# Turning 256 rows of the last layer on TensorE, and storing the last tile from ScalarE's queue

## The chip, the cores and the metric

The kernel runs on one core of a Trainium2 chip. The metric is the device time of one execution in microseconds (us); the time before is 461.48 us, the median of 3 runs (460.27 to 465.0). The core has TensorE (matmuls and weight loads, results in PSUM), VectorE, ScalarE and GpSimd (elementwise work, GpSimd also the gathers), and SyncE, which only issues transfers. Every engine works through its own queue in order and waits for others by semaphores.

## What is computed

Three layers, each working on the output of the one before. The first is a recurrent attention over 2 x 8 heads, 768 steps, with 40 channels a head. The second is a mixture of 8 experts over the 1536 tokens of 320 channels, two experts for each token. The third, the last, is a dense layer with an exponential unit:

```python
def _moe2_ref(x, w_in, w_out) -> np.ndarray:
    h = x @ w_in
    alpha = 1.0
    g = np.where(h > 0.0, h, alpha * (np.exp(np.minimum(h, 0.0)) - 1.0))
    return (g @ w_out).astype(np.float32)
```

Here x is 1536 x 320, w_in 320 x 2048 and w_out 2048 x 320, all fp32. The experts have 1024 hidden channels each and a relu.

## The kernel before

All large products are made of fp16 halves: a number is split into a high and a low part, and two or three products of parts are summed in PSUM (`PASSES`, L112, for the first matrix of a layer; L951, L952 and L954 for the second).

The attention runs in 12 tiles of 128 tokens (`attention`, L643). Each tile ends in `token_rows` (L620), which splits its rows, stores them to `x_rows` in DRAM and computes the router's logits. `router` (L771) makes tables of the rows that each expert takes. `expert` (L965) runs 16 times (8 experts, 2 halves of the tokens): gathers of rows `xg`, a turn to `xT` with channels on the partitions (`turn_row`, L587), the first product (`contract`, L938), relu and split, the second product (`second`, L940), and a store of `yo` to `y_rows`.

The last layer works on 6 blocks of 256 tokens (`last_layer`, L1130). For each block, `mixed` (L1109) takes two tiles of 128 tokens: two gathers of the experts' rows (`yg`, L1116), a weighted sum `x3` (L1121 on ScalarE, L1122 on VectorE), a split into `x3r` (`split_row`, L580: the high part L388, L389 or L391, the low part in two instructions, 64 and 256 columns, L403), and a turn into `x3T`. `ffn_in` (L1141) then multiplies by w_in, 8 groups of 16 matmuls (a pair of 128 hidden channels for 256 tokens, a PSUM bank each; three banks go round), and takes the unit on ScalarE (L1153 to L1155) and VectorE (L1156, L1157), with a split into `gh` and `gl_`. `ffn_out` (L1166) multiplies by w_out, for each tile 4 groups of 12 matmuls of 0.136 us, scales the result on VectorE (L1172, `zo`) and stores it (L1174).

Turning rows has two ways in `turn_row`. One is a transfer that transposes, on SyncE's queue (L590). The other, with `on_pe`, is five transposes of 128x128 on TensorE into a PSUM tile `T` (L594) and one copy of 128x640 into the destination, on VectorE (L378) or ScalarE (L379). The attention's tiles and the first three expert jobs take the second way, the last layer the first.

The order of the work is not that of the program text. Each call of `do` only records an operation (a group of instructions of one engine, with what it reads and writes and the engines that could do it). `do.run(ORDER)` (L1229) then issues all of them in the order of a compressed table, `ORDER` (L73 to L110), whose entries are the operation's number and which of its engines does it. Waits between engines follow from the buffers. So every engine's queue is a part of that list, and an engine that waits for one operation holds up all that stand behind it in its queue.

At the end, a flag says if the routing went over the tables' sizes; every engine loads it (L1233) and takes a branch (L1235) over a fallback, which is not run with these inputs. SyncE then waits for all transfers and engines (L1409).

Of the kernel before, what the change touches and what calls it, by code (L numbers as in the profile page):

```python
# [70 lines left out]


ORDER = """  # L73
c-jTQeFVCBf&lR6{r&y<KJVY>siC8#rJ<#vrK33w{n4G4e)LC6OFvo~IvN`KqobvvrJ<ptrJ<prqop7H(bCe;($LV-(T|pfj*gCohWmW7D1tBufkcrS5<|
LZ97!N~w2t)9B$7hXh=OF09Fj-ENDFBr5bGl)B#AbV4w6O(=ot9`%OZVrffkS`RzxCL6{#Rw^c~tmhUf_0p<{H9F0nE)K@;c-&0zzijQxPduqm3y;#dMZq
HA=4ZO{T%#Ye~qO=2tTcUTIWAa#6$t+6xO!2f}zu`6~#=SUN&;6?0;R<RrQd+dh(7s}vUY=`|X_AP2753GxbcpWQYdu)a*kRqz!DHI{r$PZWz2l&U>6MJD
c4)F$t;CHl%e}Wyc0senz3xDBLJd6`~1b?DUtd0LS#t>iOEo_Ah5rPniHa5becnt4gF(QtCi>HYlvO(Ts1EPaZkr-M+=eR<2@sEivHpYj<0-xXse2ITZ0O
EyyfsKhha$~c^3eOQX5l2VFl*kijBtZ}uf+^%0x5*8@B4)%EPZDJm5`Yx2zYrC4PE5%p{spdLJN(x;ME;0x2uP-g0ud${Y>zL9K6XL|*p^rlcVt40up*Jh
f53-WiO8Wxyi82Uf5Df?KM^x>N96DnnZ>K<37?aB@)rca_QV0%BEKR3nVev0>WqiU3tqsBWQ5F+4t7DtSRStsHS|Cni4$=qzQK;j8@x&!$Qkx~;);~WESV
!O#0{wv|4x+2zms$9N8*OJh$e9(DkOr|(K}JX?|7T3k}2x9_yftH58_F5hzA}eYvdCzpa}T~f+SxEfhuT^_#?rPG4e_-$U2#$8l*^em@d;}GSrQXlUb_I4  # L80
45G^V#dsbnKCnG&Irh_$P@XVyps>IMzyIY@+2?hN92+`Pzz?ste7>kVOHdk`VZ<;>Wb&7E(MS+BcOG9O<t%YbEX>TiK)>|dPANW20c*?`oe6<7l}|;hM>N
n8Wcens3ujU7z&^^4e2}kBA#rE5~#nCEZropRG$jdC8|sb^o<ImE%bYGKt<@!Nr*;Jg;MD|#V}2@P2QLm-KOu%gHo6W^E;|TJ}H73QZMGobjcUnCTw&>b?
7b~r2##n$JCrQD4Tjq#pnt3XBtv}q6rRR1*S(LT$~P52|7XnrbqYbDK#LMw9QQDDLtbJHc2ZS!+u46N&8HU`H=aR3NsNTMX%^NwWj;zh-{;28l@x5f)dyV
yP{&$pU4E0WKzt}RFsLLU(p}aQHtR<be4wPj!AG)F3qI5Exn`n^q$Gl2YN{f+>!o}>Yy1W%jB3mQ(#W?nNCm}D#;}&z@@k_m!}K#n);5)a2NUw^9fgCcGR
3J(ce>LMq#h?jegL-r7LuWsWNpY!o}DIbEgl?fqim6(QoM(_o7jzNH>|!nK)Nt;%tIVvNpHk2tLK8*$kUyb8Mb1utj#kmDnX$W-Dxo%W-+`#g#dfuW(hi$
`!aZ2iO`{=eFE|Tk$p4X6r1&Z}|qh<BD8^YjJ0;#~!&R*Jn4}fW2{hZpgN|2H)d4+=v~sCvL)aIg!6`Q})V@xI4Gz<9vdDa0_<M&e*^5JHE-c`97!cEgtY
ae#v(D72D;L{E)Z#6u)Q3-1q#1hkTfy^G#L}`+S;@@B==|$M_MS;ivqVKk!+e5WeJ+!h$aeGoBHa{MX!(PYJe|=hMQJ%kgFY!V5x$Zwm!JBb@j%|KN}8mC
p(}AukjJASwbBhg@B(3Nx-Kl!b{<5#I1Mp)NFpt<V&1e2KsFO|d7m*rXU1fzTJ;@-@CC41_h?5uSWkc=3o35o{qNMumqs6z0N6fb2p@iDO|YOof?{7FR+<
Y=}3ZB}T=ya1b^^R@@0k;Uwh5I=>eS(q1?V8@4IM#JK1S3GpdhgqL_?U&2**ig#fxO~jt~OCc`w#fN~1Q?bnsL_(a2Eh#TDVpuqdZLuQ?Vn;fNXYnE)#jD
sA%hF9mq>a>-%Hme)OLws-m861L6cchqs)$1oN^ixev=(DhNvuk3sV9x3urv}Q(pVfwHE}1^q`EYf=Hf;iOAC>ZQu0umNHZxeHKc_!ml)}tBuE2!C7q?Qe  # L90
32&dRT|1SNs)kLO9^2rkK}jaOukEq{GGUzH}YIw$O-8oo#glOR^G`O>C7gjm3)=c@>;&gH~B7SB|=Wh5BVuSB}92ijJ%gS>_I-5zm^19Q1;S6ddVx1P^xl
Cww0lBlp~6w9Ho;~lNlu^#gvS!$YHrI1EnlOWu#1$l@e7d@>rQFK#s_HIj$s>nUa-r@?6;}e^z$lQdui$X{T(Ij1pD~@>$s{2gQ+(N>L`%s2o)r@`bIdHz
lcLm6MWFE=o$dD-R_vrInbRS8{4o-K$rnpfu%*vSpvj&kCY8R7EW+KxI@xwN<E=l#ZNGKTsp;=Q5O&YD%ptCp9j&)P_=1>WZz!)VNw!(&|+$s$KaDIirTP
zMNG{YE$VbZMCeP)r*=}59(3<AN8(w)Sfz2*Jf9Js0Fp6LhY@JXc4Wiw&j5;XgzJDKDC<qx$;zB>R2T-M4zZ#rKil*qPEee>P+n`bFHMU)ugsj7iv`NYm7
Efx~!@VwUJiV1{%=DT1rc62koU1`b3**ZKa~Ew6!+V7TQKD>Pu~_{Y`7>F)gd@^sau^GFn{QYYFYBU9_vVR8Lw?%WF5SpaK1^J+zWu)+_o}t?Db))}h|kz
tC%XT_5Njy|3@ot-jY8UC?8CRU7MyKGY|mp^x;L-qgR=n_5_}X>t8it)WHqmbTQR`dn{oS9S(ET0&pxQ+=Ul^@E-S8IT1@{iv_?6gcT;od6g8s^|2So&z_
%tCc_+<Us)x0RyU_3@Ts>1fYPl{?PAw8_dB|CyczFGcx*1FBptb19h+f2xx#MP>j#O5v;)m0MG)!5R4vxMjxEO0OXAh*n%!7n_(krtiT!AM$t$ZF=GhAY}
$wzGvhx&1nhtfq5y)bc>!@_Z?ug)IDlV*IQYm&fH4Szl(95c#@y%_CF2Sn;9*pawXrZZ#&<?RFB@IsWbBNy(J-FiU|fu&@uQJ3YDUGV8%^T|vc}Co%)8MK
5#}HiVJl|Ocp5eHW&8{nQ#4zKZH|n-5oHw<m=QB-#!P75LD>A#h?^;MY$VLDjjWk8b7sp-n;COx<jsQl#w?kLF*WXH*Q}cxb8GI*y?HdRX4~wTJ@aAq&4&
3j2c}{Ht86#TmpL>MYiy28+nSpTvtkn#V?pZ!D`G`0!HQXJdt%0|s@=8oR>DeJDXU=B>`(2Jc{Yny$F5s_Yib^xroDI4R>tbtC2MY#t%{Yk-dZ)QZ|AJL)  # L100
3jPv!;0JQ%#}H?2KLY%*$sPWjjXoSvBp-{T38dSXSM9Tm9_8I(pp(Z>l<rrZLF=eV-MEMI$39HXI-oxEyaFX4-42YD`AiAo3*x&PR>r+w*7FR9kwGjViR`
Mj@c8NwWs#U5$uh<wfFYip4kigz4Ojq*@$ztcXr->ItM#thn<Uawf}B2&c#02H+yCh&da&m4?E-iWGjx~ylmh&4s;53*-1O7dod#p=|-KHleUMUxRdsZ_S
jiEZD-<SoUD^@l1|>qIjk$VCHqI`=A@jPS#v5*)hRe{oRYJ0rjFvq-LltpvR=ojJAJ3;G@P7gyK`9aK63^Ra9hsM3A+h*<Ya8<rre18uU^tEdTS@@rro?d
bL#Hgjky`O=oZ|n_la9}Yu+B_+~0U5ujE$T1$^t)y_VZ>n{M0fxLvpJZk(DscLwgzJ;1%Ybhl2=UAQB633txIX?UM`D|hXV-HAJOkFe#<+@rg3zjF`n+1<
HOPx0>V$$h#HH|AYj#9P6aOL&YYcvtu4p5R~LUm@_?-q`DTT`%t0-rDPUeQ)4><;}d27YU}`#Cs1n-rU=IdoSUgJ?J5D=PkVN;00dc!CQJ^FC1LFh_~{t-
rY-jH!mGLJOVQC=!Ibfo;(5m<h{HojKgS<^3re!+pr8{FaeWLfw2HU8$y_cDY%0-n1MN%hXoi9im(JLunI@;4wFG0*5DI9U;}1@Uj>NYfpNbJ75@dBumv*
#;j_Nr+dlBaKJ+7g%KwEQ^Amp3Px~1^>*s=;|8GGt7{k2ZgA-Wv>wdv6`z62OSNykr%dh!OzwP&7$DhJNPzw6~+~4~{f8-DRu|M$#@DF~^|HhyBD}U+VeI
{7=Yk%XP{D*(=xBkvQ`l&z&%0WA*1>@lCU;IkY397-5{>`rk-JlUPgH|vNdciE{2a{kB%!99jQLqT!1?%AHE5SL~1>0a1Y=V7o2#!HI^zuP~gs#CQK!Q^+
gLZHaZowmX2IWvV)C>tBCNv7Yf=Y-8wL;O55&|J2a6&K?3B^M3P$KkEC>5%PvY||<9fH9)lndoUh0vQ&DO3w}LiJE1)D87Q{}1NZS84
"""  # L110
# [1302 lines left out]
```

## Time and profile before

| | |
|---|---|
| median of 3 runs | 461.48 us (460.27 to 465.0) |
| the profiled execution, its time | 461.11 us |
| its span, first to last instruction | 459.3 us |
| TensorE matmul busy | 436.1 us (95%) |
| VectorE busy | 382.2 us (83%) |
| ScalarE busy | 299.1 us (65%) |
| GpSimd busy | 95.9 us (21%) |
| mean granted TensorE clock | 0.99 |

A row of the trace names a line of the kernel, an engine (PE is TensorE's matmuls, PEld its weight loads, DVE VectorE, ACT ScalarE, POOL GpSimd, SP SyncE; a q behind the name is the engine's queue, as DMA issues, waits and branches), the operation, the tiles it writes and reads, and shapes. Idle time in brackets stands before the row's instruction, with what ended it. A line such as L388 or L403 is that of a helper and stands for many places.

### The profile page before, as it was taken

Reading aid. Unit: us, or ns where it says so; the run is one execution under the profiler, and the core shown is the slowest. Engines: PE = TensorE matmul, PEld = TensorE weight load, DVE = VectorE, ACT = ScalarE, POOL = GpSimd, SP = SyncE. Lnnn points to the kernel's source line nnn. Section 1 sums busy time; section 2 is a strip of 40 time slices with the busy share of each in tenths; the row PEclk is TensorE's granted clock in tenths of the full one; section 3 lists DMA queues with packets and bytes.
Section 4 is the critical chain, followed back from the end, with each engine's and each line's share of the span. In section 5 each row is a group of like instructions: output and inputs, shape, how many; then the busy total and the mean of one; then the engine's idle time right before and its main releaser. Section 6 shows DMA issues by size and latency. Waiting matters only on the chain.

```text
span 459.3 us, 10628 instructions
## 1 busy us (share of the span) xinstructions
PE 436.1 (95%) x4128; PEld 369.8 (81%) x4128; DVE 382.2 (83%) x845; ACT 299.1 (65%) x525; POOL 95.9 (21%) x105
## 2 busy tenths in 40 slices
...
DMA packets 100482, 66.22 MB, mean 144 GB/s; under 512 B 76344, under 2 KB 92040, under 8 KB 100424
## 3 DMA queue, kind: packets, MB, share of 16 engines
...
q8 instruction: 34, 0.56, 0.5%
...
q10 hardware_dynamic: 64, 0.10, 0.1%
...
## 4 chain that ended last, share of the span: by engine, by line
PE 57%; DVE 17%; DMA 12%; ACT 7%; issue 4%; SPq 1%; POOL 0%; ACTq 0%; DVEq 0%
PE S L938 24%; PE O L951 8%; PE O L952 8%; PE O L954 8%; DMA sw<-in_moe_w 5%; PE O L735 4%; DVE hidden L995 2%; DVE wa L399 2%; DVE wb L399 2%; DMA sf<-in_moe_w_in 2%; DMA yg<-y_rows,rows_i 1%; DMA sf<-in_moe_w_out 1%; DMA xT<-xg 1%; DVE nm L383 1%; DVE na L1078 1%
## 5 line engine op out<-in xcount | busy, mean ns | idle before, releaser
L938 PE MATMUL S<-xT,wa 128*128 128x224 f16 (+1 forms) x1024 | 99.4, 256 | 1.1 <-DMA xT<-xg 0.8
L938 PEld LDWEIGHTS <-wa 128*128 128x128 f16 x1024 | 93.7, 99 | 4.2 <-DVE na L1078 1.0
L938 PE MATMUL S<-x3T,fwa 128*128 128x256 f16 x768 | 88.3, 273 | 2.9 <-DMA x3T<-x3r 2.9
L938 PEld LDWEIGHTS <-fwa 128*128 128x128 f16 x768 | 75.1, 98 | 13.2 <-issue 3.2
L951 PE MATMUL O<-wb,hidden 128*128 128x320 f16 (+1 forms) x256 | 75.3, 299 | 1.4 <-ACT yo L379 0.6
L952 PE MATMUL O<-wb,hidden 128*128 128x320 f16 (+1 forms) x256 | 75.2, 299 | 0.0
L974 POOL DMA_INDIRECT xg<-x_rows,table x32 | 36.8, 1149 | 127.1 <-DMA xT<-xg 104.9
L954 PE MATMUL O<-wb,hidden 128*128 128x320 f16 (+1 forms) x200 | 59.8, 299 | 0.0
L951 PE MATMUL O<-fwb,gh 128*128 128x320 f16 x192 | 57.4, 299 | 0.0
L952 PE MATMUL O<-fwb,gh 128*128 128x320 f16 x192 | 57.4, 299 | 0.0
L1156 DVE SCALAR_TENSOR_TENSOR ex<-ex,th 128x512 f32<-128x512 f32 x48 | 32.9, 688 | 19.7 <-ACT ex L1154 10.0
L995 DVE SCALAR_TENSOR_TENSOR hidden<-S,hidden 128x128 f16<-128x128 f32 (+2 forms) x92 | 39.9, 455 | 3.9 <-ACT hidden L993 3.6
L993 ACT ACTIVATE hidden<-S 128x448 f16<-128x448 f32 (+1 forms) x64 | 32.0, 510 | 15.0 <-PE S L938 14.9
L1153 ACT ACTIVATE th<-S,sca 128x512 f32<-128x512 f32 x48 | 32.9, 687 | 11.7 <-PE S L938 11.6
L1154 ACT ACTIVATE ex<-S,sca 128x512 f32<-128x512 f32 x48 | 32.4, 685 | 11.2 <-PE S L938 11.2
L1155 ACT ACTIVATE re<-S,sca 128x512 f32<-128x512 f32 x48 | 32.8, 691 | 10.7 <-DVE gl__6001 L399 3.2
L1116 POOL DMA_INDIRECT yg<-y_rows,rows_i x24 | 26.3, 1098 | 49.6 <-DVE x L1122 23.1
L1157 DVE SCALAR_TENSOR_TENSOR re<-ex,re 128x512 f32<-128x512 f32 x48 | 34.2, 712 | 2.9 <-ACT re L1155 0.8
L952 PEld LDWEIGHTS <-hidden 128*128 128x128 f16 (+1 forms) x256 | 26.8, 105 | 9.4 <-issue 2.5
L1072 ACT ACTIVATE nm<-sf 128x320 f32<-128x320 f32 (+1 forms) x28 | 16.2, 577 | 27.6 <-DVE fwb L399 10.0
L951 PEld LDWEIGHTS <-hidden 128*128 128x128 f16 (+1 forms) x256 | 26.8, 105 | 7.0
L399 DVE SCALAR_TENSOR_TENSOR wa<-sw,wa 128x1024 f16<-128x1024 f32 x24 | 28.9, 1218 | 0.6 <-ACT wa L388 0.6
...
## 6 DMA issues: line engine op xcount, KB each, us to landing
...
```

The lines of the kernel that those rows point to most:

```text
L399: some(on, [("V", 0.07 + 0.06 * m + 1.04e-3 * n, lambda: V.scalar_tensor_tensor(dst(), src(), scale(), hi(), op0=OP.mult, op1=OP.subtract) ...
L938: PE.matmul(acc, wa[:, r, w, f * P:(f + 1) * P], xT[:, j, :n], start=(i == 0), stop=(i == 7))
L951: PE.matmul(o, a, wb[:, 0, f % FB], start=(f == 0), stop=False)
L952: PE.matmul(o, a, wb[:, 1, f % FB], start=False, stop=(not b and f == last))
L954: PE.matmul(o, b[0], wb[:, 0, f % FB], start=False, stop=(f == last))
L974: do([("G", 1.1, lambda: G.indirect_dma_start(out=xg()[:n], out_offset=None, in_=(x_all if hf else x_rows[0]())[:, :], in_offset=bass.Indi ...
L995: vec(2 * n, lambda x=x, n0=n0, n=n: V.scalar_tensor_tensor(hi(x, n), src(n0, n), 0.0, hi(n0, n), op0=OP.max, op1=OP.subtract), [ph, hid[f ...
L1153: act(512, lambda: A.activation(th(), pf(), AF.Tanh, scale=sca()[:, 2:3]), [pf, sca], [th], "exp", 1)
L1154: act(512, lambda: A.activation(ex(), pf(), AF.Exp, scale=sca()[:, 1:2]), [pf, sca], [ex], "exp", 1)
L1155: act(512, lambda: A.activation(re(), pf(), AF.Relu, scale=sca()[:, 1:2]), [pf, sca], [re], m=1)
L1156: vec(512, lambda: V.scalar_tensor_tensor(ex(), ex(), 1.0, th(), op0=OP.add, op1=OP.mult), [ex, th], [ex], port=True)
L1157: vec(512, lambda: V.scalar_tensor_tensor(re(), ex(), 0.0, re(), op0=OP.min, op1=OP.add), [ex, re], [re], port=True)
```

## The change

The turn of the first block of the last layer (b = 0, two tiles of 128 tokens) takes the way over TensorE. The store of the very last tile (t = 11) is issued from ScalarE's queue, all other stores of the output still from SyncE's. Since the first edit makes two operations of each of two, there is a new `ORDER` table for 2027 operations instead of 2025.

```diff
 ORDER = """
-c-jTQeFVCBf&lR6{r&y<KJVY>siC8#rJ<#vrK33w{n4G4e)LC6OFvo~IvN`KqobvvrJ<ptrJ<prqop7H(bCe;($LV-(T|pfj*gCohWmW7D1tBufkcrS5<|
...
+c-jTQeFVCBf&lR6<@>z9KhO7hf2pOVqoE%S4GsNhXz6I_Xy|BYX=rI^X=!Nb=xAtYY3PrJmWGCgj)sngj)s<ohK_DE^ha}AS~^-<?(;zqfYgy58b_i?3`r
...
@@ -1122,7 +1122,7 @@
             split_row(xr, x3, None, [x3])
-            turn_row(xr, P, xT, n0, [xr], [xT[n0]])
+            turn_row(xr, P, xT, n0, [xr], [xT[n0]], not b)
@@ -1171,7 +1171,7 @@
             t = 2 * b + i
-            load(lambda: [(out[t * P:(t + 1) * P], zo())], [], [zo])
+            load(lambda: [(out[t * P:(t + 1) * P], zo())], [], [zo], q="SP" if t < NT - 1 else "A")
```

Read out of the new table, beside the old one. The two groups of transposes stand directly ahead of the last 12 matmuls of the last expert job; behind these comes the first group of the last layer. In the old table the 12 matmuls came ahead of that group with nothing between. The first tile's copy is VectorE's, the second's ScalarE's. In VectorE's queue, one of the first tile's two low parts (the 64 columns) stands between the high part and the low parts of the second tile, and the copy behind them. The four gathers of that block stand in the same order as before. ScalarE's store is the last in its queue. Beyond that, most operations of all queues stand a few places earlier or later than before, in every part of the kernel, and some have another of their possible engines; the first of the filling groups (three matmuls on constants, L513) stands 30 places later in TensorE's queue.

## Rows read from the trace of the kernel before

**Rows 1.** Busy time of each engine by stretch: start:end, length, busy us (instructions), granted clock.

```profile
0.00:100.00 100.00, 89.16 (x1101) 77.65 (x1102) 90.06 (x288) 82.91 (x152) 32.25 (x44) 0.97 0.83 171
100.00:288.00 188.00, 184.46 (x1685) 160.68 (x1682) 164.81 (x337) 109.84 (x194) 39.11 (x36) 1.00 0.85 223
288.00:291.10 3.10, 0.24 (x2) 0.03 (x1) 1.83 (x7) 0.56 (x1) 1.21 (x2) 1.00 0.64 155
291.10:453.40 162.30, 162.24 (x1344) 131.42 (x1344) 124.94 (x216) 105.78 (x178) 23.31 (x24) 1.00 0.17 40
```

**Rows 2.** TensorE's timeline around its long wait: start us, us, instruction [idle before it].

```profile
286.45 0.30 PE L951 MATMUL O<-wb,hidden 128*128 128x320 f16 x1
...
287.94 0.30 PE L954 MATMUL O<-wb,hidden 128*128 128x320 f16 x1
291.10 8.89 PE L938 MATMUL S<-x3T,fwa 128*128 128x256 f16 x80 [2.86 <-DMA x3T<-x3r]
```

**Rows 3.** Chain that ended last, 279 to 291: start us, us, what.

```profile
279.77 6.62 DMA yg<-y_rows,rows_i x2
...
287.44 0.57 DVE x3r L403 x2
...
288.03 2.94 DMA x3T<-x3r
```

**Rows 4.** SyncE's queue in the timeline, at the hole and at the end.

```profile
284.61 4.62 SPq L590 DMA_TRANSPOSE x3T<-x3r  x2
...
452.33 1.96 SPq L369 DMA_DIRECT2D out<-zo  x2
```

**Rows 5.** TensorE's timeline: transposes and expert matmuls at both levels of the clock.

```profile
10.53 0.31 PE L697 MATMUL T<-id,k 128*120 128x128 f16 x1
...
12.13 0.31 PE L698 MATMUL T<-id,q 128*120 128x128 f16 x1
...
81.69 0.44 PE L594 MATMUL T<-id,xr 128*128 128x128 f16 x5
81.97 0.44 PE L594 MATMUL T<-id,xg 128*128 128x128 f16 x5
...
88.28 4.56 PE L938 MATMUL S<-xT,wa 128*128 128x192 f16 x32
...
93.26 1.48 PE L938 MATMUL S<-xT,wa 128*128 128x192 f16 x16
```

**Rows 6.** Copies of turned rows out of PSUM: ns of one, min/median/max, first and last start.

```profile
L379 ACT ACTIVATE xTt<-T x10: 686/700/723, 36.3 to 86.5; 128x640 f16<-128x640 f16 x10
...
L378 DVE COPY xTt<-T x2: 482/483/484, 46.7 to 87.3; 128x640 f16<-128x640 f16 x2
```

**Rows 7.** ScalarE's timeline around the hole.

```profile
286.96 0.56 ACT L1121 ACTIVATE x<-yg,cw 128x320 f32<-128x320 f32 x1 [2.44 <-DMA yg<-y_rows,rows_i]
...
293.05 0.69 ACT L1153 ACTIVATE th<-S,sca 128x512 f32<-128x512 f32 x1 [3.02 <-PE S L938]
```

**Rows 8.** VectorE's timeline, its last instruction.

```profile
453.38 0.55 DVE L1172 TENSOR_SCALAR zo<-O,sca 128x320 f32<-128x320 f32 x1 [1.08 <-PE O L954]
```

**Rows 9.** Transfers issued in the first 3 us, ScalarE's queue: ns of one.

```profile
L369 ACTq DMA_DIRECT2D gf<-in_f_gate x1: 442/442/442, 0.8 to 0.8; - x1
```

**Rows 10.** The closing branch (L1235), by queue: ns min/median/max, first and last start us.

```profile
L1235 SPq EVENT_SEMAPHORE  x8: 17/17/17, 457.1 to 457.6; - x8
L1235 ACTq COMPARE_BRANCH  x1: 50/50/50, 447.4 to 447.4; - x1
...
L1235 ACTq EVENT_SEMAPHORE  x1: 17/17/17, 450.1 to 450.1; - x1
...
L1235 SPq COMPARE_BRANCH  x1: 58/58/58, 454.3 to 454.3; - x1
...
L1235 DVEq EVENT_SEMAPHORE  x1: 21/21/21, 457.3 to 457.3; - x1
```

**Rows 11.** The closing waits after it (L1409), SyncE's queue.

```profile
L1409 SPq EVENT_SEMAPHORE  x14: 17/28/28, 457.7 to 459.3; - x14
```

More of the change, by code (lines that the diff above doesn't have):

```diff
@@ L73 @@
 ORDER = """
[L74 to L108, printed above, removed]
@@ L109 @@
-gLZHaZowmX2IWvV)C>tBCNv7Yf=Y-8wL;O55&|J2a6&K?3B^M3P$KkEC>5%PvY||<9fH9)lndoUh0vQ&DO3w}LiJE1)D87Q{}1NZS84
+c-jTQeFVCBf&lR6<@>z9KhO7hf2pOVqoE%S4GsNhXz6I_Xy|BYX=rI^X=!Nb=xAtYY3PrJmWGCgj)sngj)s<ohK_DE^ha}AS~^-<?(;zqfYgy58b_i?3`r
+naw1#xiB$7v4ND4_K8KjLg5D)7kX*7v;kSro2Ii!U2kO5ji`e+gP1s1`gSQuHLd1Q-Lks&%lzeUSP1=*ovbcv0T6*@r&$R5pMKcWdVhLy43U~6=PPSGPeL
+MBKai(?6FfhDmjc0w1(25TZ!e1%=GHTDg9!?xJ_SOxzrmd0rOiZ$>vTE{Qw72RPo<ZE<~{S7N%MNGiwNEfMNMf69^LLOKNYvMAVLT@O<8`u%6;X|Z_BVd3
+}aT>AkJNm?4n1?s9F#ap-g(En?X;4DHzyaXF|DhjXE$oT5@iz7~-oYdI8d)I&Fhxdq45YyaV2At<*1>+lVrUni<9kE~Q5=FXo&`51hIg?AJ_2z(2PXIuU*
@@ new lines @@
+UNWM=dY}GLgVv=o>Hw7V#NYMiFd{e~tregHOQ>Z1EL1BMAVBB=`*f4)B<V%)th1kR9%UBwj(ML<;n=0`Q3U@h})*dtAY2EQfAE8qeTA;tOy>Cd3d+5hLu5
+6u~dS1e8FYfY?8Qx5N^$v40_|Xqr6YJ5UA{umlD4FZi4|AbW7Z&-et(;b9_+Z;=^s07q~F1w2EX!B<!ft%3+qB(g+_m|<h=L;M1M3%<e1L>>GN<cJG$MDj
+R-HbD#AkOOhUOL&F&Z{mUc3~t~K%J?16pl$jI9-sprcpd$B@OS(~AjB1k5<LKjD)Bj>i3PzE9Xdv&$SirqGh~;p5k2}{B1hJVI04Wr(Wh(Vk{HlKdPI-u2
+|cA}^qgMMOL|4G>Aw;$q)om@@W`Eb5Dfw%KM|jh7h*#n$$ule<cc_uPvT6TNExkDTlz>hsS~{>8t9q6kQ?GcKam%~qg&!iBP2v?RGy^KFnXgKWP<|aoi31
+{ku+H(TWAvn6i+runtC!N@&}?tHVKRJsXr5K&?m2CnG92(5^W+v@zig~8%fi5(nANNOg`ub*`nH%g+9p+^`u{PhZvGwVnphsMUF{@8c|&e(2%+_ACnQ(BP
@@ new lines @@
+V2!no}|zrD7Cd5hhIbh!=yfJpCWkk^&4$#i>4(pkClhYDFcfH8mjqLDI|@L=>Hp7VXn1DndefLZzt~J*D2zVLC$3sISQ#{YUD-%*h2Qvk@dgC+R4iqG|RE
+s)NSJKH;%Z@&hWtuE-6wrFPVwI#6krXO<+-rs)j5r?YgHYNJPLMC9l^y&<>cnmkcs;!M3Eb5xSeuwnLBY=TU&7wSE-K<~&8=_p&E@>GesQ6+j$mgy@cGap
+e8szMd181r|kLRaYsTcbaw>U4vCQ3xGlA={+q?5FgBezI{k&Lo&5bEhm8a49CuWSA_IWAaRaDKa&-&X$-mvtSQQg{d-27BV%a!Is!ETVb25#jMyhn`86ri
+`}v<_Q0atircYmmgWkqz@6DTvtg@jgDJ8-rq6WPEq7!G%$^-GBj&`8nG1Vkdu*JOxdeA-A=hOm%$1!o4X(*O*fzId=1hy5F*|O=cDOG01GnbFT!ibhOJ>C
++x&PvNT%Q}W7MJ3poX72%AvfYCT$7n|vT$V5T!x!+18%{^IKUscF*jh7{EVadBUj>=T$cM2o8vP4l;!yppXN`TC1iOh<oG-{WG~#AYx7qw&wGN*7x)`j<q
@@ new lines @@
+KSys|!WG#^1RQxiVkj>wJTMa1{>nPj1Fmxe4Fodwf%<aV@^j5BM$L;p<#OcyV2R$d7o0FL6mBB}DkJVDV8tBRqsT-x6;8m|yTye#S5Ph_K?<d|Ej08~(^g
+g%iKyW5S+4^LrsHT=;^R6Pn^nxbkr!A^7~AfAH_{Yw^jy__lxuK<Eh*p)cfxrx52m0wc7<flwBBp(CCIM4Sp|;UXM_zPM(N!d18l8)hSh`L3`PXF^$QF?X
+TO6ojHs5sG3$Dv3j(B38wb&=to*Pi%`H3j+~|bD<<eMNgzfUL1*2aV^Bep?G4#VnkdB8(}Oi#FVrX<Kj#lNHuXT*2Rf<7887j8A}&Y7QYoHQc}8#4e?uXD
+c!`W1Vu|+i9=~5ourwxk<t<(0qJ|;E`B2|q=c9elVVofN_+7k?xdBpmY!lwxJrBJEZrnp;-!mpmtNvSI!I5cD!n8`K8QzgB>?$-k(X=INwnml9FdPwMk-0
+PEX#H2pT(VUW@ITQXC)|?rLY90l^l_xa$cIqo;;Fs(p0WUV|gae<*mGv7xGe$%NaQ#hvmI&OKW)}ALO&VWe!F`I?6>UE#73HM3uUdluvS2zQ|E2CN-72e3
@@ new lines @@
+c(^Uc4|l<thI|&dHwCP*O6Y&<d~Ym4?)jWTh#k<+YKQyHY`}$WXBqPe~{q^9v=Sw3L_<SK`vAQc_7NY2~Ce<f3v_igHOQD<#=dd&)uSNmaQf*X6R@lsj@;
+39CaTqhyu5Qc#XcTRJNjrLVN)hf+~)%0Rg*eF;%LwWExbh{~&DWukQDuJTk~%3P@`H3g_W^{GyknSyAa$#b=+cA1UVmlw)fNvcD&q?Xl@N~>+TuMX6KEUR
+O6qJE{W)Ra0?p}JNN>O$S9X?3Z-)QXx>w<^%i>P3yJ8>Oi2)V<o$uIjf+OpU8uEurqT@0Fu^Qg3Qj9cWNnDLFN-{!M+T1+}78)uu{oC2az$T3M@UpJ-d{c
+Un^mGnVFQ5oWBlwVu||`r2L_YBe>iMYK=UhRSQQHqmC<NLy-At)<4aw%SpXT3kzL2W_s+;8a^^|EcYiBs^+s?W8@lly=dw+FLCJ(=Y?GFbDIn088+!wc%9
+*FsIGo6axLJ-L$**(quiSS78n2wIa-D!%#s-U>RN+8uG9Lp<ag(2;mww;P2rAwxA57a06+*2m5dUyQ-%zA+N7s2j=xIEb3+B2ramUVLhrRbW4xuLpXvS9K
```

12 lines of the change are left out of this document (added).

## Prediction

> **What bounds the kernel now.** I read the stretches first, then TensorE's own timeline around its one long wait, then the chain of waits there, and last the closing instructions of each engine.
>
> The stretches say which engine sets the pace where [rows 1]. From 291.1 to 453.4 us TensorE is busy for 162.24 of 162.30 us, at a granted clock of 1.00, and VectorE for only 124.94: the last layer costs exactly its matmuls, and nothing that VectorE or ScalarE does there shows. From 100 to 288 it is busy for 184.46 of 188, so 3.54 us are idle. In the first 100 us it is busy for 89.16 and VectorE for 90.06, and the clock averages 0.97: this is the only part where the engines wait for each other in turn (10.84 us of idle TensorE). Between 288 and 291.1 TensorE does nothing but wait. From 453.4 to the end of the span at 459.3 it has no work at all. So a change can gain in four places: the first 100 us, the 3.5 us scattered over the experts, the hole of 2.86 us before the last layer, and the 5.9 us after the last matmul.
>
> The hole: the last group of 12 expert matmuls starts at 286.45, one every (287.94 - 286.45) / 11 = 0.1355 us, so 12 take 1.63, and the first matmul of the last layer waits 2.86 us, until 291.10, for the transfer that turns the rows [rows 2]. The chain of waits says what is late [rows 3]: the gathers of the experts' rows take 6.62 us, VectorE finishes the split row of the second 128 tokens at 287.44 + 0.57 = 288.01, and the turning transfer takes 2.94 us from there, with 0.13 us more to the matmul. SyncE's queue issued the two transfers within 4.62 us from 284.61 on [rows 4]; the first was early, only the second counts.
>
> **The change part by part.** *Turning on TensorE.* Removed: two turning transfers on SyncE's queue; what stood behind them there is a store that the order places later and that waits for other work, so freeing the queue is worth nothing by itself. If that cover were gone, it would be worth at most the 4.62 us in which both were issued and waited for [rows 4]. Added: twice five transposes and a copy out of PSUM. Five transposes of this shape take 0.44 us, and the next five begin 0.28 us after the first (81.97 - 81.69), so 0.056 us from one to the next; the 16 at the start come 0.107 us apart ((12.13 - 10.53) / 15) [rows 5]. By these the first stand at the higher and the last at the lower of the clock's two levels, 2.4 and 1.2 GHz. The copy of 128x640 takes 0.483 us on VectorE and 0.700 on ScalarE [rows 6]; the new table puts the first tile's on VectorE, the second tile's on ScalarE.
>
> The place decides more than the price. In the new order both groups of transposes stand ahead of the last 12 expert matmuls, and the first matmul pair of the last layer behind these. So TensorE, which before ran the 12 from 286.45 on, now stops at the second group until the split row is complete; queued behind it are the 12 and everything later. VectorE's new order also puts the small rest of the first tile between the steps of the second tile: half of the two instructions' 0.57 us [rows 3], 0.28. Step by step: split row 288.01 + 0.28 = 288.29; semaphore 0.10 (between the 0.02 and the 0.13 of the chain); transposes 0.44: 288.83; then the 12 matmuls, 1.63: 290.46. Meanwhile ScalarE copies: 288.93 + 0.70 = 289.63, hidden under the 12 with 0.8 us to spare. ScalarE is free for it: the last gathered tile that stands ahead of it there was scaled at 286.96, and it waited 3.02 us before 293.05 [rows 7]. The pair starts at about 290.5 instead of 291.1: **-0.6 us**. The 2.94 us of the transfer do not come back whole, because the cover was moved behind the wait. Bounds: with no delay on VectorE and a hop of 0.02, 290.10, so -1.0; if the clock fell to its lower level in that wait, transposes and matmuls both at half speed (0.88 + 3.26 instead of 0.44 + 1.63), +1.5. I hold the upper bound for unlikely: the wait of 2.86 us before left the granted clock at 1.00 [rows 1, 2], and the new one, from 286.45 + 0.44 to 288.39, is shorter.
>
> A rule that speaks against this edit is in the Trainium skill, VectorE: DVE Perf Modes, section "The three transpose paths": 390 ns for one 128x128 turn on TensorE against 1309 ns by DMA. By 390 ns each, five would cost 1.95 us, an estimate from that page, and the pair would start near 292.0, 0.9 us later than before. The trace shows turns that overlap at 0.056 us, so I do not follow it.
>
> *The rest of the last layer.* TensorE has no idle time there now [rows 1], so the pull ahead of 0.6 us goes through to the end if no new wait arises. The two copies fall before VectorE's and ScalarE's work there starts.
>
> *The last store from ScalarE's queue.* The last tile is scaled until 453.38 + 0.55 = 453.93 [rows 8], and SyncE has issued both last stores by 452.33 + 1.96 = 454.29 [rows 4]; ScalarE's issue at the start took 0.44 [rows 9]. The store does not queue now, since SyncE is free when it comes. But after its last instruction every engine takes a branch over the fallback code, and the next instruction follows late: on SyncE the branch is at 454.3 and the next at 457.1; on ScalarE 447.4 and 450.1; VectorE goes on at 457.3 [rows 10]. SyncE then passes eight waits until 457.6 and fourteen more from 457.7 to 459.3 [rows 11]. With the store gone, SyncE's last one is that of the tile before, issued at 452.33, so it is through its branch (2.8 us) and its eight waits before VectorE is. Then VectorE at 457.3 is the last, with ScalarE at 453.95 + 0.44 + 2.7 = 457.1 just ahead: SyncE's closing waits run from about 457.3 instead of 457.7: **-0.4 us**. Bounds: -0.8 if a quarter of the fourteen waits' 1.6 us is passed early as well; 0 if ScalarE's branch comes back 0.6 us slower than its own of before. ScalarE has nothing after the store.
>
> The Trainium skill says against it (Trainium Kernel Development and Optimization, Key Constraints) that issuing from several engines saves only the sequencer's issue time. The store is not queued behind another issue, so by that rule this edit gives 0 and the total would be -0.6, a time of 460.9. The row with the branch is why I count 0.4.
>
> *The new order table.* Read out of the two tables, 232 of 354 TensorE groups, 320 of 467 ScalarE, 620 of 764 VectorE and 150 of 235 SyncE operations stand elsewhere, but by 1.4 positions on average (VectorE 2.9), and 41 operations go from VectorE to ScalarE, about as many the other way. Where TensorE is saturated this costs nothing: its own queue covers it, and if that cover goes, it costs the wait itself. In the first 100 us it can go either way. Above: all 10.84 us of idle time, of which the first few are the load of the gates, so I count a third, 3.6 us, as the bound of a gain; below: as much again as a loss, since the same chains are only shuffled. I take **0**, the middle, because nothing in the rows favours a side.
>
> Sum: -0.6 - 0.4 + 0 = -1.0. The profiled execution took 461.11 us, its span 459.3 and 1.8 around it; -1.0 gives 460.1. It lies 0.37 below the median of the runs, 461.48, so on their scale the forecast is **460.5 us**.
>
> **The rivals.** *The shuffle gains.* If the early part gives back its third, 3.6 us, and the rest is as above: 456.9. For it: idle time of 10.84 us is there, and VectorE and ScalarE trade work evenly. Against: VectorE is busy 90% of that stretch, so little can be moved forward.
>
> *The clock rises later at the start (slower than before).* Place: TensorE's first microseconds. In the new order the first of the filling groups (three matmuls on constants, before the gates) stands thirty groups later. The transposes from 10.53 to 12.13 run at the lower level now, those at 81.69 at the higher [rows 5]. If what came before them made the clock rise, it now comes later. The nearest price is the other stretch at the lower level: 32 matmuls in 4.56 us, where 16 take 1.48 at the higher, so 4.56 - 2.96 = 1.6 us lost [rows 5]. Less 1.0: 462.1. It decides once the loss is over 1.0 us. A second dip like that would give 463.7. For it: a clock of 0.97 over the first 100 us [rows 1] shows that it can be low there. Against: the other filling groups stay.
>
> *The change does not do what it says.* TensorE stops for the split row and gains nothing at the hole (if the gathered rows or the copy on ScalarE come 0.6 us later than reckoned), and the store gives nothing: 461.5. For it: the copy stands behind another gathered tile on ScalarE; if that tile's rows land 0.8 us after the reckoned copy start, the pair waits. Against: it was there at 286.96, two microseconds early [rows 7].
>
> **How the numbers follow.** The forecast as reckoned, 459.5 to 461.2: 0.40. The shuffle gains, 455.5 to 459: 0.26. Nothing of it, 461 to 462: 0.14. The clock or another early wait costs, 462 to 464: 0.13, and more than that, up to two such stretches and a stalled chain: 0.07. The range for 8 in 10 leaves out the last and half of the gains' lower part: 456.0 to 464.0. The likeliest one's own range is 459.5 to 461.2. One per cent is 4.6 us, about what a measurement of this kernel (460.27 to 465.0 in three runs) can tell from no change. Faster than 456.9 takes the better half of the shuffle's gains, 0.15; slower than 466.1 the worst tail, 0.07; within it, 0.78.
>
> **What would show it right or wrong.** In the profile after: TensorE's wait before the transposes of the split row near 1.5 us, five transposes in 0.44 to 0.5, then twelve matmuls and no wait before the first pair, which starts 0.5 us before 291.1 less what the early part moved; two turning transfers fewer (10 of the 12); no wait of TensorE after that; SyncE's branch about 1.3 us ahead of VectorE's. From the first pair to the last matmul, 162.3 us again. If that stretch is longer, a new wait arose in the last layer and the step "goes through to the end" fails. If the first pair comes 3 us earlier or later than 290.5, the shuffle, not the turning, made the result.

## The result: 0.6% slower

The changed kernel takes 465.32 us (median of 18 runs, 462.14 to 468.31). The kernel before, run beside it, takes 462.72 (18 runs). The ratio is 1.0062, 95% interval [1.0038, 1.0086], so the change costs 1.8 to 4.0 us, where the prediction had a gain of 1.0. The ratio is over fast runs alone; two of the runs of before, 469.02 and 896.89 us, are not among them. On the scale of the three runs shown ahead of it, 461.48 x 1.0062 = 464.3, just above the range.

The stretches of the changed kernel (start:end, length, busy us of TensorE, its weight loads, VectorE, ScalarE and GpSimd, granted clock, DMA share, GB/s), which answer to [rows 1]:

```profile
0.00:100.00 100.00, 87.08 (x1068) 75.99 (x1068) 89.40 (x280) 79.03 (x144) 32.40 (x44) 0.93 0.81 164
100.00:288.00 188.00, 181.64 (x1672) 157.66 (x1671) 165.01 (x339) 112.93 (x195) 33.75 (x31) 1.00 0.85 222
288.00:292.00 4.00, 4.00 (x32) 3.38 (x30) 2.90 (x7) 2.12 (x5) 2.84 (x3) 1.00 0.46 128
292.00:457.00 165.00, 165.00 (x1373) 133.79 (x1371) 127.13 (x221) 109.64 (x184) 25.93 (x28) 1.00 0.18 42
```

The hole is gone: TensorE works through from 288 to 457. The idle time came earlier: 12.92 us in the first 100 where it was 10.84, at a clock of 0.93 instead of 0.97, and 6.36 us from 100 to 288 where it was 3.54. TensorE's timeline at the place of the edit (start us, us, instruction), which answers to [rows 2]:

```profile
292.59 0.30 PE L954 MATMUL O<-wb,hidden 128*96 128x320 f16 x1
292.73 0.72 PE L594 MATMUL T<-id,x3r 128*128 128x128 f16 x10
293.29 0.30 PE L951 MATMUL O<-wb,hidden 128*128 128x320 f16 x1
...
294.78 0.30 PE L954 MATMUL O<-wb,hidden 128*128 128x320 f16 x1
294.92 0.27 PE L938 MATMUL S<-x3T,fwa 128*128 128x256 f16 x1
```

Ten transposes in one run, no wait, the 12 matmuls, and the first pair at once. But it starts at 294.92, 3.8 us later than in before. VectorE's low parts there (the small one of the first tile and both of the second):

```profile
292.07 0.72 DVE L403 TENSOR_TENSOR x3r<-x,x3r 128x64 f16<-128x64 f32 x3
```

The split row is complete at 292.79, 4.8 us later than in before, and the second five transposes start at 293.01. So the row itself is late here, and TensorE comes just behind it.

To place the loss I use TensorE's lateness: the time at which a profile's timeline has issued as many matmul columns as before had at a given time, less that time (matmuls on constants and the new transposes left out). In the changed kernel it is 1.3 us at 75 us, 4.8 at 100, 5.3 at 110, 5.0 at 160, 6.8 at 288, and 3.8 from 300 to the end. (Where two kernels order their work differently, the figure moves by up to a microsecond with the point that is taken.) So most of the loss is made in the first 110 us, and the closed hole gives 3 us of it back.

### The profile page after: what moved, and what is told of

It reads as the page before. It is cut to its first block, busy times and chain, and to the rows that moved or that the text cites. A ratio compares the mean times of both kernels' runs of the same rounds, so it can differ in the third digit from the quotient of the medians.

```text
span 463.4 us, 10658 instructions
## 1 busy us (share of the span) xinstructions
PE 437.9 (95%) x4138; PEld 370.8 (80%) x4138; DVE 385.0 (83%) x844; ACT 303.7 (66%) x527; POOL 94.9 (20%) x106
## 4 chain that ended last, share of the span: by engine, by line
PE 53%; DVE 22%; DMA 12%; ACT 6%; issue 4%; SPq 1%; ACTq 0%; DVEq 0%
PE S L938 26%; PE O L951 8%; PE O L952 8%; PE O L954 8%; DMA sw<-in_moe_w 5%; DMA sf<-in_moe_w_in 4%; DVE wa L399 3%; DVE hidden L995 2%; DVE wb L399 2%; DMA x_rows<-xr 1%; DVE nm L383 1%; DVE na L1076 1%; DVE pw L702 1%; DVE xr L399 1%; ACT wa L388 1%
## 5 line engine op out<-in xcount | busy, mean ns | idle before, releaser
L938 PE MATMUL S<-xT,wa 128*128 128x224 f16 (+1 forms) x1024 | 101.2, 257 | 4.2 <-DVE hidden L995 2.6
```

Of the source, the lines that this page charges most:

```text
L938: PE.matmul(acc, wa[:, r, w, f * P:(f + 1) * P], xT[:, j, :n], start=(i == 0), stop=(i == 7))
```

## The experiments

Each time is compared with the kernel before on the same chip. A position is a place in the list `ORDER`.

| run | what it is | median us | ratio to before, 95% |
|---|---|---|---|
| e1 | new table, no edit | 469.35 | 1.0140 [1.0095, 1.0184] |
| e2 | turning alone, old table | 459.62 | 0.9940 [0.9916, 0.9965] |
| e3 | turning alone, behind the 12 | 459.93 | 0.9939 [0.9912, 0.9965] |
| e4 | store alone, old table | 462.90 | 1.0002 [0.9969, 1.0035] |
| e5 | new table up to 560 | 467.39 | 1.0124 [1.0101, 1.0148] |
| e6 | new table, 560 to 940 | 465.86 | 1.0076 [1.0047, 1.0105] |
| e7 | new table from 940 | 463.33 | 1.0042 [1.0016, 1.0068] |
| e8 | whole change, old table up to 940 | 459.81 | 0.9953 [0.9930, 0.9976] |
| e9 | hole filled with matmuls | 460.31 | 0.9961 [0.9929, 0.9994] |
| e10 | new table up to 280 | 465.88 | 1.0086 [1.0055, 1.0118] |
| e11 | new table, 280 to 560 | 463.83 | 1.0042 [1.0012, 1.0072] |
| e12 | turning on both sides of the 12 | 459.66 | 0.9937 [0.9908, 0.9965] |
| e13 | changed kernel, five products moved | 465.42 | 1.0074 [1.0043, 1.0104] |
| e14 | changed kernel, router's waits filled | 465.29 | 1.0073 [1.0042, 1.0105] |
| e15 | e12 with those waits filled | 460.24 | 0.9958 [0.9929, 0.9986] |

### The parts one by one

e1, the table without the edits:

```diff
-ORDER = old
+ORDER = [the new table; each pair of transposes and copy is the old turning transfer]
```

> The new order table alone: the rows of the first 256 tokens are turned by transfers and the last tile is stored from SyncE's queue, as before, each in the place that the new table gives the edit. Theory T (the table costs the time): TensorE falls 4 to 5 us behind before within the first 105 us, as it does in the changed kernel, and the end comes 2.5 to 4.5 us later than before, 0.5 to 0.9%. Rival R (the two edits cost it, the table nothing): within 0.6 us of before. If the time lies at half of the changed kernel's loss, both have a part.

e2, the turning without the table (in `ORDER`, five transposes and a copy stand where each turning transfer stood):

```diff
-            turn_row(xr, P, xT, n0, [xr], [xT[n0]])
+            turn_row(xr, P, xT, n0, [xr], [xT[n0]], not b)
```

> The old table with the turning on TensorE alone: both groups of five transposes take the places of the two turning transfers, ahead of the last 12 expert matmuls, as in the changed kernel; the store stays on SyncE. Theory T, by the steps of the prediction: split row at 288.0 to 288.3, first pair of the last layer near 290.5 instead of 291.1, so 0.6 us faster (bounds 1.0 faster to 1.5 slower). Rival R: 1 to 3 us slower.

e3, as e2, with one more move:

```diff
-ORDER = [..., transposes 1, copy 1, transposes 2, copy 2, ..., last 12 expert matmuls, ...]
+ORDER = [..., last 12 expert matmuls, transposes 1, copy 1, transposes 2, copy 2, ...]
```

> As the run with the turning alone, but the last 12 expert matmuls stand ahead of the first five transposes. They end at 288.18 while the split row is complete at 288.0 to 288.3; then come transposes of 0.44, a copy of 0.70 on ScalarE and two hops of 0.1 each, so the first pair starts near 289.5, 1.6 us ahead of before and 1.0 ahead of the run with the 12 behind the wait. If where the 12 stand does not matter, it is as fast as that run.

e4, the store alone:

```diff
-            load(lambda: [(out[t * P:(t + 1) * P], zo())], [], [zo])
+            load(lambda: [(out[t * P:(t + 1) * P], zo())], [], [zo], q="SP" if t < NT - 1 else "A")
```

> The old table with the last output tile stored from ScalarE's queue alone. By the prediction SyncE's closing waits run 0.4 us earlier: 0.4 us faster. By the tail of the changed kernel (last matmul to end of span 6.2 us instead of 5.9, ScalarE's closing branch 458.7 and its next instruction 462.4): 0.3 us slower, with 3.7 us between that branch and ScalarE's next instruction instead of 2.7.

The parts add up: 1.0140 x 0.9940 x 1.0002 = 1.0081, against 1.0062 [1.0038, 1.0086] for the whole. The table is what costs, about 6.5 us, more than the 2.5 to 4.5 of theory T; rival R falls. The turning gains 2.8 us, more than expected, and where the 12 matmuls stand cannot be told apart. The store's effect cannot be told from 0 by its time.

In e2's profile the turning looks like this. TensorE:

```profile
285.06 0.44 PE L594 MATMUL T<-id,x3r 128*128 128x128 f16 x5
286.33 0.88 PE L594 MATMUL T<-id,x3r 128*128 128x128 f16 x5 [0.82 <-DVE x3r L389]
287.05 0.30 PE L951 MATMUL O<-wb,hidden 128*128 128x320 f16 x1
...
288.68 0.49 PE L938 MATMUL S<-x3T,fwa 128*128 128x256 f16 x3
```

and VectorE:

```profile
285.95 0.33 DVE L389 TENSOR_SCALAR x3r<-x 128x320 f16<-128x320 f32 x1
286.31 0.56 DVE L403 TENSOR_TENSOR x3r<-x,x3r 128x64 f16<-128x64 f32 x2
```

TensorE does not wait for the whole split row. The transposes of its high part start at 286.33, as soon as the high part is there (285.95 + 0.33), while VectorE still makes the low part; the five are spread over 0.88 us because the later ones wait for it. The wait is 0.82 us, not the 1.5 of the prediction. TensorE was 1.4 us early at 280 in this profile, before any edit could act, and 2.4 early at 300, so the hole gave 1.0; in e3 the same difference is 0.7 + 0.8 = 1.5, in e12 1.7. The runs gain 1.6 to 3.9. What is the rest?

### What a hole costs besides its length

The windows behind the hole (start:end, length, TensorE's busy us, granted clock, DMA share, GB/s), in before:

```profile
292.00:296.00 4.00, 4.00 (x39) 1.00 0.33 102
```

in e4, where the same hole stands:

```profile
288.00:292.00 4.00, 1.15 (x10) 1.00 0.63 154
292.00:296.00 4.00, 4.00 (x24) 0.57 0.33 93
```

and in e5:

```profile
292.00:296.00 4.00, 2.13 (x11) 0.63 0.53 146
296.00:300.00 4.00, 4.00 (x21) 0.52 0.14 41
```

At a clock of 0.57 four microseconds hold 24 matmuls instead of 39. In four of the seven profiles with a hole of 2.9 to 3.4 us (e1, e4, e5, e10; not before, e7, e11) the clock stood at 0.5, its lower level, for 3.4 us at the end of the hole or behind it, in e5 for 6.8. (So it did in e6, whose profile is of its slowest run and is not counted.) Half of that is lost: (3 x 3.4 + 6.8) / 7 / 2 = 1.2 us on average, or 1.1 without the 1.9 us of it that lie still within the holes. In the eight profiles without a hole (after, e2, e3, e8, e12 to e15) the clock never stood at 0.5 there. Whether the two are tied was tested by e9, which leaves the hole's length as it is and has TensorE work in it:

```diff
     judge()
+    for _ in range(6):
+        te(3, 384, lambda: [PE.matmul(bank[:, :384], ones16(), ones16()[:, None].to_broadcast([P, 3, P]),
+                                      start=True, stop=True) for _ in range(3)])
     do.run(ORDER)
```

with the six groups behind the last 12 expert matmuls in `ORDER`.

> The kernel before, with 18 matmuls on constants (six groups of three, 0.48 us a group, 2.9 us in all) put behind the last 12 expert matmuls: TensorE still waits for the turned rows, but works meanwhile; the last layer starts at the same place. In four of six profiles with a hole of 2.9 to 3.4 us the granted clock fell to 0.5 around its end, for 3.4 us (three) or 6.8 us (one); in the four without a hole it did not. Theory K (the hole costs its length and the lower clock behind it, on average (0 + 0 + 3 x 3.4 + 6.8) / 6 / 2 = 1.4 us): 1.4 us faster than before, 0.3%, no lower clock behind the hole. Rival N (the lower clock behind the hole is chance and is not tied to it): within 0.4 us, with a lower stretch there in about two of three profiles.

It is 0.39% faster [0.06, 0.71], 1.8 us, and its windows are:

```profile
288.00:292.00 4.00, 4.00 (x29) 1.00 0.88 190
292.00:296.00 4.00, 4.00 (x36) 1.00 0.38 104
```

The clock stayed at 1.00, but so it did behind three of the seven holes, and the lower end of the gain, 0.3 us, is within rival N's 0.4. The mean granted clock of the whole execution, which is on record for every run, says more. The 12 runs of e9 have 0.988 to 0.995, mean 0.9915; the 35 of before beside them 0.980 to 0.994, mean 0.9877, and 20 of them have 0.987 or less. The difference, 0.0038 of 461 us, is worth 1.75 us, about the gain. This is what theory K asks for and rival N does not, though a mean does not say where in the run the clock was low. e2, e3 and e12, which close the hole, have means of 0.9891 to 0.9899 against 0.9876 and 0.9877, worth 0.7 to 1.1 us.

So the hole of [rows 2] cost on average its 2.86 us and, as an estimate from these figures, about a microsecond more, which the one profile of before did not show. With it the gain of the turning would be 1.0 to 1.7 + 1.1 = 2.1 to 2.8 us, and 2.8 (1.6 to 3.9) was measured. e12 puts five transposes on each side of the 12 matmuls and both copies on VectorE:

```diff
-ORDER = [..., transposes 1, copy 1, transposes 2, copy 2 on ScalarE, ..., last 12 expert matmuls, ...]
+ORDER = [..., transposes 1, copy 1, last 12 expert matmuls, transposes 2, copy 2 on VectorE, ...]
```

> The old table with the turning on TensorE, the first five transposes ahead of the last 12 expert matmuls and the second five behind them, both copies on VectorE (0.48 us instead of 0.70); the store stays on SyncE. Split row about 288.0, the rest of the transposes 0.2, copy 0.48, three hops of 0.1: the first pair near 289.0, 2.1 us ahead of before by the hole alone, and no lower clock behind it: 0.6 to 0.8% faster. If the hole alone counts, 0.45%.

At 0.9937 it is inside the intervals of e2 and e3. These three beat both kernels of the case.

### Where in the table the loss lies

e5 to e7 and e8, e10, e11 take the order of operations from the new table in one part of the list and from the old in the others. As one line, for e5:

```diff
-ORDER = old
+ORDER = new[:560] + [x for x in old if x not in new[:560]]
```

The expectations placed the cuts too early. By the logits and the expert matmuls in the trace, position 280 is at about 43 us, 560 at 81 and 940 at 162.

> The kernel before, no edit, with the order of the new table for the first 560 operations (TensorE's first 62 us or so) and the old order for all the others. The new table alone cost 6.5 us (1.4%); in its trace TensorE is 1.9 us behind before after 60 us, 5.1 after 100, 6.5 after 140 and 7.6 at the end. Theory F (the start pays it: fewer chains in flight while the attention runs): 2 us slower here, and what follows grows from it to the full 5 to 6. Theory D (it is spread as the lag is): 2 us slower, the middle 3 to 4, the late part 1. Theory L (the start is caught up, as TensorE waits for the experts' rows anyway): within 0.7 us of before.

> The old order for the first 560 operations, the order of the new table until 940 operations are placed (TensorE from about 62 to 137 us: the end of the attention, the router, the first experts), then the old order again. Theory D: 3 to 4 us slower. Theory F: within 0.7 us. Theory L: the whole 6 us.

> The old order for the first 940 operations, the new table's from there on (TensorE from about 137 us: the other experts and the last layer, where it is saturated), with 75 of the 95 operations that change their engine; the rows are turned by transfers and the store is SyncE's. All of theories F, D and L: 0 to 1 us slower. If it costs over 2 us, saturation is no cover.

> The changed kernel with both edits and its own table from operation 940 on, but the old order for the first 940 (until about 137 us). If the loss of the new table lies ahead of 137 us, the time is that of the turning alone, 459.6 us or 0.6% faster than before; the store adds nothing. If the late part of the table costs something too, between that and before.

The start alone costs 1.24%, nearly the table's 1.40, as theory F has it. But the middle put in alone costs 0.76, 3.5 us, as theory D has it, where theory F allowed 0.7 us; and the late part costs 0.42, 1.9 us, where all three allowed 0 to 1. So no theory fits all three runs. The three do not add up to the whole (2.42): this would follow if a TensorE that is already late no longer pays for later waits, as it does not for the hole, but no run tests it. e8 shows it from the other side: the complete change with the old start and middle is 0.47% faster than before.

The start does not lose all of its 5 us where it stands. In e5's profile TensorE is 4.6 us late at 110, 2.5 at 288 and 5.7 at 300: more than half of the last figure comes at the hole, behind which the clock stood at 0.5 for 6.8 us.

> The old order with the new table's order for the first 280 operations alone (until about 33 us), where the first filling group moves thirty places back and VectorE is idle 0.99 us longer within 24 us. Theory P (VectorE's waits for GpSimd's instructions, 3.7 us until 84 us in the new table's start and 2.0 in the old, and that idle time, set the loss): 1 to 1.5 us slower, one long VectorE instruction (0.49 us) added. Rival S (the start-up decides all): 5 us slower.

> The old order with the new table's order for operations 280 to 560 alone (about 33 to 62 us). Theory P: the VectorE instructions that stand long beside GpSimd's come to 3.0 to 3.3 us until 84 us instead of 2.0, TensorE is 1 to 1.5 us late at 75 us, the run 1 to 3 us slower. Rival S: within 0.7 us of before.

e10 is 4.0 us slower where theory P had 1 to 1.5. Part of that is its own seam: TensorE waits 2.35 us at 51.6 behind a load of k that lands late, which is not in e5. So the two halves do not tell how the 5 us are shared out.

### VectorE beside GpSimd, and TensorE's clock

In the first 100 us VectorE is the busiest engine, and its records show one thing that makes it slower in the new order. In the changed kernel, VectorE:

```profile
57.52 0.48 DVE L399 SCALAR_TENSOR_TENSOR q<-qt,q 128x320 f16<-128x320 f32 x1
57.92 1.15 DVE L399 SCALAR_TENSOR_TENSOR k<-kt,k 128x320 f16<-128x320 f32 x1
```

and GpSimd:

```profile
57.63 1.09 POOL L383 TENSOR_TENSOR yb<-y,sg 128x320 f32<-128x320 f32 x1 [2.41 <-DVE sel L803]
```

Two instructions of one shape: 0.48 us, and 1.15 when it starts beside GpSimd's product, which ends at 58.72; the longer one ends 0.35 after that. The Trainium skill, SBUF — State Buffer, section "SBUF: two separate sides", says that the port pair that VectorE and GpSimd share is locked for a whole instruction and the other one blocks; the trace agrees, 0.67 us added over an overlap of 0.8. Until 75 us before has four such instructions (0.2 us or more above the median of their like), with 2.0 us above it; the changed kernel has eight with 3.9. The ten profiles that start in the old order have four, or six (e6 and e9), with 1.9 to 3.1 us; the four that start in the new one without another edit there (after, e1, e5, e14) have eight each, with 3.9 to 4.1. The lateness at 75 us is less clear-cut: 0.8 early to 2.4 late in those ten, 1.3 to 2.1 late in these four.

The sum of this excess and of VectorE's idle time from 5 us on follows the lateness at 75 us: 0.8 less in e2 and e12 (0.8 early), 0.5 more in e4 (0.45 late), 1.6 more in e9 (1.6 late), 1.9 more in e5 (2.0 late); in the changed kernel 1.4 more (2.0 of excess, 0.5 less idle), 1.3 late. It fits e11 least (1.0 more, 0.5 late). Since VectorE's work until there is nearly the same in all, this is in part bookkeeping; the test is to take such meetings away. e13 moves five of the products:

```diff
-[y0, sg], [y], on=ON["y"])
+[y0, sg], [y], on="V" if t in (0, 4, 6, 8, 9) else ON["y"])
```

> The changed kernel, with the gate products of five token tiles (the 1st, 5th, 7th, 9th and 10th) moved from GpSimd to VectorE. In the changed kernel VectorE has eight instructions until 76 us that take 4.0 us longer than their like, each beside a GpSimd instruction; five of them, 3.1 us in all, stand beside these five products; before had four with 2.0. Theory P (these waits slow VectorE, which paces the stretch): five products of 0.45 us are added to VectorE, 2.3, and 3.1 go, so TensorE is 0.8 us less late at 75 us (0.5 instead of 1.3) and the run 0.5 to 1 us faster than the changed kernel. Rival W (work moved to the busiest engine costs its time; the long instructions lay in idle time): TensorE 3 us or more late at 75 us, the run 1.5 to 2.5 us slower than the changed kernel.

The place behaves as theory P says: four long instructions are left until 75 us, with 1.7 us, and TensorE is about 0.1 us late at 75 us instead of 1.3, although the busiest engine was given five more instructions. Yet the run is no faster (1.0074 against 1.0062, the intervals overlap). At 100 us it is 3.2 late instead of 4.8, at 110 both are over 5 late. The chain that ended last shows what takes it back. It goes through the experts' weights, and there through the eighth load of its kind from the start. Before, whose chain goes through the ninth, this load's split is, in ScalarE's timeline:

```profile
105.88 1.06 ACT L388 ACTIVATE wa<-sw 128x1024 f16<-128x1024 f32 x1 [0.24 <-DMA sw<-in_moe_w]
```

The changed kernel's chain:

```profile
92.32 8.78 DMA sw<-in_moe_w
...
105.70 5.79 DMA sw<-in_moe_w
...
111.51 1.07 ACT wa L388
```

e13's chain:

```profile
103.95 7.23 DMA sw<-in_moe_w
...
111.21 1.06 ACT wa L388
```

The experts' weights are staged. VectorE's split of one load frees the buffer of the next. In e13 this load is released 1.75 us earlier, takes 1.44 longer and lands within 0.3 us of the same time. So here the weights are late, 5.6 us behind before in the changed kernel (111.51 against 105.88) and 5.3 in e13, about as late as TensorE. The load ahead of it is split at 104.20 in before and from 103.5 to 105.7 in eight of the other nine profiles with the old start, at 109.1 to 109.8 in the changed kernel, e1 and e5, and at 107.93 in e13. That VectorE's lateness is one cause of this is argued from the chain; e13 shows that these five products are not enough to mend it.

The other suspect was the clock: in the changed kernel it is at 0.5 from 86.6 to 96.8 us, in before from 85.1 to 91.9. (It is also at 0.5 from 52.4 to 55.9 us, but so it is near there in e3 and e8, which are faster than before.) e14 and e15 put matmuls on constants into TensorE's waits for the router, as e9 does (`range(6)` and `range(4)`).

> The changed kernel, with six groups of three matmuls on constants (0.48 us a group at the higher clock) put on TensorE ahead of the logits and transposes that it waits for between 83.4 and 90.7 us (3.1 us of waits). Theory C (those waits let the clock fall to 0.5 from 86.6 to 96.8, and the expert matmuls from 90.9 on pay half of 5.9 us for it): no or a shorter low stretch there, 1.5 to 3 us faster than the changed kernel, so about as fast as before. Rival N (the clock falls there whatever TensorE does): 0 to 1 us slower than the changed kernel.

> The old table with the rows turned on TensorE, five transposes on each side of the last 12 expert matmuls (0.63% faster than before), and four of the same groups on constants between 82.8 and 88.0 us. In before the clock is at 0.5 from 85.1 to 91.9 us, of which the expert matmuls from 88.3 on pay 1.6 us. Theory C: 0.8 to 1.6 us faster than the run without them, 0.8 to 1.0% faster than before. Rival N: 0 to 0.8 us slower than the run without them.

Windows of e12 (columns as in the first fence):

```profile
84.00:92.00 8.00, 6.64 (x65) 5.75 (x63) 6.91 (x22) 5.56 (x13) 3.92 (x4) 0.64 0.77 225
92.00:100.00 8.00, 8.00 (x98) 7.00 (x96) 7.62 (x24) 6.39 (x10) 0.00 (x0) 0.93 0.73 198
```

and of e15:

```profile
84.00:92.00 8.00, 6.91 (x103) 5.76 (x102) 6.20 (x18) 5.76 (x14) 4.35 (x4) 1.00 0.74 214
92.00:100.00 8.00, 5.55 (x60) 4.67 (x57) 7.66 (x27) 5.96 (x11) 0.00 (x0) 0.81 0.72 177
```

In e15 the clock stays at 1.00 until 92, and TensorE is 1.2 us early at 95. Then it waits, in e15 (waits from 92 to 120: who for whom, us in total, times, longest):

```profile
PE bank L810 <- DVE sel L803: 2.5, 1, 2.5
PE S L938 <- DVE hidden L995: 0.7, 1, 0.7
```

At 100 us it is 2.1 late, and the clock was at 0.5 from 97.0 to 100.4. In e14 the wait is again one for VectorE (its lines stand one further down):

```profile
PE S L939 <- DVE hidden L996: 3.0, 2, 2.7
```

Both are no faster than without the filling (1.0073 against 1.0062, 0.9958 against 0.9937), although the mean granted clock of their runs is higher: 0.9903 in e14 against 0.9854, 0.9942 in e15 against 0.9899, worth 2.3 and 2.0 us. So theory C falls: there the lower clock lies in time that TensorE would spend waiting for VectorE. It counts behind the hole, where TensorE sets the pace.

## Why the prediction was wrong

**Failed: the order table at 0.** The bounds of plus and minus 3.6 us were drawn from 10.84 us of idle time, and the middle was taken because "nothing in the rows favours a side". The table costs 6.5 us (4.4 to 8.5), beyond the bound, and e5 shows that its start alone costs nearly as much. The sum could not be right without it. What the runs show in its place: TensorE is 5.3 us late at 110, the experts' weights are split about 5 us later, and VectorE's instructions that stand long beside GpSimd's go from four to eight. The bound reckoned with TensorE's idle time only, whereas in that stretch VectorE is the busiest engine and its own instructions can grow. And a shuffle of 620 of 764 VectorE operations was counted as neutral, though the old order has only four such instructions, so that there was more to lose than to win; this is argued, since e13 took them away without a gain. "Where TensorE is saturated this costs nothing" fails too: e7 changes the order from 164 us on alone and costs 0.42% [0.16, 0.68].

**Mis-sized: the hole, -0.6.** The sign and the mechanism were right, and so was "the 2.94 us of the transfer do not come back whole". The term measured 2.8 us (1.6 to 3.9). Two pieces were missing: the transposes of the high part start before the split row is complete (a wait of 0.82 us, not 1.5), and behind a wait of 2.9 us the clock was often down. The prediction saw the clock only as a risk of the new order and held it unlikely because one profile showed 1.00 behind the hole. In four of seven it was at 0.5. (The small rest of the first tile delays VectorE by 0.17 us in the changed kernel, 292.07 to 292.24, not by 0.28.)

**Failed: the store, -0.4.** Its time, 0.9969 to 1.0035 of before's, cannot tell -0.4 from 0; the closing of the trace can. In e4 the closing branch and what follows it are, by queue (ns, first and last start us):

```profile
L1235 SPq EVENT_SEMAPHORE  x8: 17/17/17, 457.5 to 459.2; - x8
...
L1235 SPq COMPARE_BRANCH  x1: 57/57/57, 454.9 to 454.9; - x1
L1235 DVEq COMPARE_BRANCH  x1: 72/72/72, 456.2 to 456.2; - x1
L1235 ACTq COMPARE_BRANCH  x1: 54/54/54, 457.1 to 457.1; - x1
...
L1235 DVEq EVENT_SEMAPHORE  x1: 21/21/21, 459.1 to 459.1; - x1
L1235 ACTq EVENT_SEMAPHORE  x1: 17/17/17, 460.4 to 460.4; - x1
```

SyncE is 1.3 us ahead, as reckoned (454.9 against VectorE's 456.2). But ScalarE takes its branch 0.56 us after its store was issued (456.16 + 0.38) and comes back 3.3 us later, not 2.7, and so it is last, 1.3 us after VectorE. The gap moved to the other engine. This is the case for which the prediction itself had 0, "if ScalarE's branch comes back 0.6 us slower than its own of before". From the last scaling (L1172) to the end of the span it takes 5.7 us in e4 and 6.0 to 6.8 in the four other profiles with ScalarE's store (after, e8, e13, e14); with SyncE's it is 5.9 in before and 5.8 to 6.3 in the others, so nothing is gained there. The rule of the Trainium skill on issuing from several engines (Trainium Kernel Development and Optimization, Key Constraints) is that it saves only the sequencer's issue time; by it this edit gives 0, and the runs agree.

**Right:** from the first pair to the end of the last matmul 162.2 us (294.92 to 456.86 + 0.30); no wait of TensorE in the last layer; transposes 0.056 us apart (ten in 0.72), so the row of the trace was the better price; copies hidden. The Trainium skill's 390 ns for each turn (VectorE: DVE Perf Modes, "The three transpose paths") would be 3.9 us for the ten, an estimate; the trace shows 0.72 and decides. "If the first pair comes 3 us earlier or later than 290.5, the shuffle, not the turning, made the result" is what happened: it came 4.4 us later.

**The rivals.** "The clock rises later at the start" had the sign, but neither the size (462.1, or 463.7 with a second dip, against 464.3) nor the place: in the changed kernel the first transposes come 0.107 us apart until 11.20 and 0.055 from 11.65 on, where before has 0.107 until 12.13 [rows 5], so the higher level comes earlier, and TensorE is 0.6 us early at 15. "The shuffle gains" got 0.26 and the wrong side of the same term 0.20.

**Open.** Which of the reordered operations makes the weights 5 us late at 110 us is not settled: SyncE's queue, the splits that free the staging buffers and the length of the transfers all changed together. The first split of weights on ScalarE is the largest shift, at 68.62 us where before has 59.63; but e11 has it too (67.81) and costs only 0.42%. Nor is it settled why the middle and the late part of the table cost 0.76 and 0.42% when put in alone.
